# Preparing q and k of a head pair in one 128-partition cast, with both low parts on GpSimd: causal attention plus gated MLP

## The chip, the cores and the metric

One NeuronCore of a Trainium2 chip (trn2) runs the whole program. The metric is the device time of one execution in microseconds (us), here the median of three runs. TensorE is called PE, VectorE DVE, ScalarE ACT, GpSimd POOL, and SyncE, which issues all of this kernel's transfers, SP.

## The reference

Inputs are q, k, v of 8 batches x 8 heads x 576 positions x 64, a row s per head, and four MLP arrays. Cut to what matters:

```python
scores = 1/sqrt(D) * q @ k.T                        # per head, 576 x 576
cum  = np.cumsum(np.maximum(s, 0), axis=-1)
bias = -(cum[:, None] - cum[None, :])
scores = np.where(causal, -1e9, scores + np.minimum(bias, 0))
attn = softmax(scores);  x = attn @ v               # heads joined: 576 x 512 per batch
h = relu(x @ w_in);  u, g = halves(h)               # 512 -> 2 x 512
g = (g - mean(g)) / sqrt(var(g) + 1e-6)             # per position
g = w_spatial @ g + b_spatial[:, None]              # over positions, 576 x 576
out = (u * g) @ w_out
```

## The kernel before

The work is cut into 32 pairs of heads (four pairs to a batch) and eight batches of MLP. All products are done in fp16 with a value split into a high part (a cast) and a low part (value minus high part), and two or three products summed in PSUM.

**A pair's scores.** For each of the two heads PE multiplies two stacked operands of 128 rows: KA with QA, and KB with QB. Each has room for three pairs at a time (QA[i], KA[i], QB[i], KB[i], i = p % 3). Before the change QA[i] and KA[i] hold, in rows 64 to 127, the high parts of q and k, and in rows 0 to 63 the constants and three prefix rows (`cum`, split into three fp16 rows `cc`) that carry the bias; KB[i] holds the low part of k in rows 0 to 63 and the high part of k in rows 64 to 127, QB[i] the high part of q and the low part of q. The function `prepare` (L367 to L401 before the change) fills them: `load` brings k and q of a pair in one transfer (k in rows 0 to 63, q in rows 64 to 127 of `raw`, room for two); `kh` casts k on DVE (L390), `kl` subtracts on DVE (L408), `qh` casts q on ACT (L411), `ql` subtracts on POOL in four pieces (L394); `ka`, `kb` and `qb` are transfers from SBUF to SBUF that move a high part to the other half of the partitions (L404, L406, L412); `aux` puts the prefix rows in rows 61 to 63 of KA[i] with three transfers (L398). Pairs 0 to 2 are computed in fp32 from raw tiles (`native_*`) and use none of this.

**The rest of a pair** (`attend`). Scores arrive in seven PSUM banks in turn (three buffers `psS`). For each block DVE adds the mask and takes the row maximum (L462), ACT takes the exponential (L479), DVE forms the reciprocals of the row sums (L484, L485), ACT writes the high part of the scaled weights (L510), DVE the low part (L512), SP transposes the result by DMA (L519), and PE multiplies with v (L618, L625). The last 64 positions of both heads (the tail rows) share two blocks, columns 4 and 9 of the row maxima; a DVE instruction joins their two maxima (`tail_min`, L489), another their sums (`tail_sum`, L493), with reciprocals of their own.

**The MLP of a batch** (`mlp`): five gate products `vps` (L668), eight `ups` (L761), eight `sps` (L776 to L779), eight `ops` (L805), each with casts on ACT and DVE between. The inverse root of the variance is taken on POOL in two instructions (L692, L693).

**What sets the order.** Nothing is ordered by hand. Every step is added to a planner (`Plan`) with its engine, a duration, a place (a number by which ready steps of an engine are picked), what it needs, and the buffers it takes and gives. `Plan.order` plays the program through with these numbers and emits each engine's instructions in the order that comes out; each engine, SP's queue among them, then runs its list strictly in that order.

Of the kernel before, what the change touches and what calls it, by code (L numbers as in the profile page):

```python
# [27 lines left out]
class Plan:  # L28
# [17 lines left out]
    def order(self):  # L46
        import heapq
        steps, index = self.steps, self.index
        n = len(steps)
        left, users = [0] * n, [[] for _ in range(n)]  # L50
# [15 lines left out]
        dma = 0.0  # L66
# [3 lines left out]
        while len(out) < n:  # L70
            for e, heap in ready.items():
# [71 lines left out]
def attn_gated_mlp(ctx, tc, kqT, v, s, w_in, w_spT, b_sp, w_out, outT):  # L143
    nc = tc.nc
    P = 128
    NHB, D, H, S = kqT.shape
# [85 lines left out]
    def load_s():  # L232
        t = wk.tile([NH, 4 * S], F32, tag="u", bufs=1, name="cst")
        cst["raw"], cst["pos"], cst["cum"], cst["zer"] = (t[:, i * S:(i + 1) * S] for i in range(4))
        nc.sync.dma_start(out=cst["raw"], in_=s)

    add("s", SYNC, 650, -30, load_s, take=["u"], move=(0, 300))
    add("zero", DVE, 400, -29, lambda: nc.vector.memset(cst["zer"], 0.0), need=["s"])

    def prefix(k):  # L240
# [80 lines left out]
    for c in range(KC):  # L321
        for hf, at, at2 in ((1, 2.2 + 1.2 * c, 6.5 + 0.5 * c), (0, 4.5 + c, 9 + 0.5 * c)):
# [4 lines left out]
        convert(("out", c), w_out[c * P:c * P + P], wo1[:, c], wo2[:, c], "wst", "ob", 10.6 + 1.1 * c, 10.6 + 1.1 * c)  # L327

    def spatial(c):
# [11 lines left out]
        at = 11 + 0.4 * c if c < NFULL else 13  # L341
# [7 lines left out]
    def bias_rows(k):  # L349
        if k == 0:  # L350
            hold["bf"] = wk.tile([1, S], F32, tag="ob", bufs=room["ob"], name="bf")
            hold["bp"] = wk.tile([1, 3, S], F16, tag="wst", bufs=1, name="bp")
            nc.sync.dma_start(out=hold["bf"], in_=b_sp)
            return
        bf, bp = hold["bf"], hold["bp"]
        if k == 1:
            nc.vector.tensor_scalar(bf, bf, SWSP * SVN / 2048.0, None, op0=ALU.mult)
            for i in range(3):
                nc.vector.tensor_copy(bp[:, i], bf)
                if i < 2:  # L360
                    nc.vector.tensor_tensor(out=bf, in0=bf, in1=bp[:, i], op=ALU.subtract)
        else:
            for i in range(3):
                nc.sync.dma_start(out=wx2[TAIL + i:TAIL + i + 1], in_=bp[:, i])

    add("bf", SYNC, 650, 13.1, lambda: bias_rows(0), take=["ob", "wst"], move=(0, 100))
    add("bp", DVE, 2800, 13.2, lambda: bias_rows(1), need=["bf"], give=["ob"])  # L367
    add("bx", SYNC, 1950, 13.3, lambda: bias_rows(2), need=["bp", ("sl", NFULL)], move=(1300, 100), give=["wst"])

# [7 lines left out]

    def prepare(p):
        i = p % 3
        lo, hi = slice(0, 64), slice(64, 128)  # L380
        set_free = [("static", i)] + ([last(p - 3)] if p - 3 >= NNAT else [])

        def load():
            raws[p] = wk.tile([P, 2, S], F32, tag="raw", bufs=2, name=f"raw{p}")
# [504 lines left out]
```

## Time and profile before

| what | value |
|---|---|
| three runs | 726.39, 728.44, 728.59 us (median 728.44) |
| the profiled execution | 728.78 us, of which the span of its instructions is 727.0 us |
| mean granted PE clock | 0.931 of full speed |
| busy share of the span | PE 83%, DVE 88%, ACT 71%, POOL 23% |
| DMA | 72.0% of 16 engines' time, 114.81 MB |

The busy share is an average over the span, which has three stretches: up to about 200 us, in which weights are converted and PE often waits; a steady stretch, in which a batch repeats every 78.6 us; and the end, in which only the MLP is left. How the profile is read: busy time of PE is modelled from when matmuls issue; DVE and ACT are busy or idle as recorded.

### The profile page before, as it was taken

Reading aid. Unit: us, or ns where it says so; the run is one execution under the profiler, and the core shown is the slowest. Engines: PE = TensorE matmul, PEld = TensorE weight load, DVE = VectorE, ACT = ScalarE, POOL = GpSimd, SP = SyncE. Lnnn points to the kernel's source line nnn. Section 1 sums busy time; section 2 is a strip of 40 time slices with the busy share of each in tenths; the row PEclk is TensorE's granted clock in tenths of the full one; section 3 lists DMA queues with packets and bytes.
Section 4 is the critical chain, followed back from the end, with each engine's and each line's share of the span. In section 5 each row is a group of like instructions: output and inputs, shape, how many; then the busy total and the mean of one; then the engine's idle time right before and its main releaser. Section 6 shows DMA issues by size and latency. Waiting matters only on the chain.

```text
span 727.0 us, 15919 instructions
## 1 busy us (share of the span) xinstructions
PE 606.4 (83%) x5696; PEld 417.0 (57%) x5696; DVE 636.6 (88%) x1669; ACT 518.5 (71%) x1319; POOL 165.8 (23%) x217
## 2 busy tenths in 40 slices
PE   1654469647889989989889988999889988999998
PEld 0232335425656766567546765667647754777676
DVE  7999999999999998899889999999899989884531
ACT  3867777775686887787776879787777779765322
POOL 8120222202224210521124221422223122200200
PEclk9966669957999999999989999999999999999999
DMA  8896967489596789859785779968895866445001
GB/s 222 240 252 126 200 117 193 111 202 200 139 191 161 145 173 189 209 124 192 173 194 119 139 189 199 191 132 183 174 225 128 193 120 150 92 94 135 22 13 65
DMA packets 243037, 114.81 MB, mean 158 GB/s; under 512 B 213471, under 2 KB 226957, under 8 KB 242958
## 3 DMA queue, kind: packets, MB, share of 16 engines
q1 hardware_dynamic: 242958, 113.80, 72.0%
q8 instruction: 44, 0.72, 0.4%
q14 instruction: 35, 0.29, 0.1%
HBM read 37.28 MB, written 9.44 MB: 64 GB/s over the span
## 4 chain that ended last, share of the span: by engine, by line
PE 28%; DVE 25%; ACT 3%; issue 3%; POOL 1%; DMA 0%; DVEq 0%; ACTq 0%; POOLq 0%
PE ops L805 7%; PE ups L761 6%; DVE pb L512 6%; PE vps L668 5%; DVE psS L462 5%; PE sps L776 3%; PE psS L456 3%; DVE KB L408 2%; PE av L618 1%; DVE V L585 1%; DVE g L796 1%; DVE g L784 1%; ACT p L479 1%; DVE sm L484 1%; DVE mx L462 1%
## 5 line engine op out<-in xcount | busy, mean ns | idle before, releaser
L394 POOL TENSOR_TENSOR QB<-raw,QA 64x288 f16<-64x288 f32 x116 | 111.8, 993 | 327.0 <-ACT QA L411 280.6
L479 ACT ACTIVATE p<-psS,mx 128x128 f32<-128x128 f32 (+3 forms) x256 | 132.9, 524 | 57.4 <-DVE mx L462 55.0
L462 DVE CUSTOM_DVE_ANT_0 psS<-psS,mb 128x128 f32<-128x128 f32 (+1 forms) x320 | 154.9, 500 | 15.4 <-PE psS L456 10.4
L510 ACT ACTIVATE pb<-p,sm 128x384 f16<-128x384 f32 (+3 forms) x256 | 123.1, 554 | 21.1 <-issue 9.9
L456 PE MATMUL psS<-KA,QA 128*128 128x128 f16 (+1 forms) x348 | 83.6, 315 | 63.0 <-ACT p L479 62.7
L512 DVE SCALAR_TENSOR_TENSOR pb<-p,sm,pb 128x384 f16<-128x384 f32 (+3 forms) x256 | 129.8, 558 | 5.1 <-ACT pb L510 4.9
L805 PE MATMUL ops<-g,wo 128*128 128x288 f16 x768 | 106.8, 296 | 3.5 <-ACT ob L812 2.4
L668 PE MATMUL vps<-win,xt 128*128 128x512 f16 (+1 forms) x576 | 102.2, 356 | 4.8 <-ACT xt L634 3.6
L776 PE MATMUL sps<-ws,vn 128*128 128x288 f16 x768 | 104.6, 286 | 0.0
L761 PE MATMUL ups<-xt,win 128*128 128x288 f16 x768 | 102.1, 286 | 2.5 <-ACT u L766 2.4
L805 PEld LDWEIGHTS <-wo 128*128 128x128 f16 x768 | 77.2, 101 | 30.8 <-issue 5.5
L456 PE MATMUL psS<-KB,QB 128*128 128x128 f16 (+1 forms) x348 | 90.0, 313 | 2.8 <-DMA KB<-kh 2.8
L761 PEld LDWEIGHTS <-win 128*128 128x128 f16 x768 | 73.8, 98 | 27.9 <-issue 6.4
L776 PEld LDWEIGHTS <-vn 128*128 128x128 f16 x768 | 74.1, 98 | 23.3 <-issue 2.1
L668 PEld LDWEIGHTS <-xt 128*128 128x128 f16 (+1 forms) x576 | 48.4, 104 | 57.1 <-issue 10.9
L618 PE MATMUL av<-pT,V 128*64 128x128 f16 (+2 forms) x960 | 68.2, 297 | 14.4 <-DMA pT<-pb 14.4
L618 PEld LDWEIGHTS <-V 128*64 128x64 f16 x960 | 53.9, 120 | 33.5 <-issue 20.8
L456 PEld LDWEIGHTS <-QB 128*128 128x128 f16 x348 | 30.1, 104 | 61.2 <-issue 55.8
L692 POOL TENSOR_SCALAR rs<-mv 128x1 f32<-128x1 f32 x40 | 15.7, 393 | 195.3 <-DVE mv L688 194.8
L479 ACT ACTIVATION_READ_ACCUMULATOR p<-psS,mx 128x1 f32 x256 | 51.0, 199 | 0.0
L456 PEld LDWEIGHTS <-QA 128*128 128x128 f16 x348 | 29.8, 104 | 34.1 <-issue 27.0
L462 DVE DVE_READ_ACCUMULATOR2_ANT mx<- 128x1 f32 x320 | 45.0, 141 | 0.0
(82 smaller groups left out, 857.6 us busy)
## 6 DMA issues: line engine op xcount, KB each, us to landing
raw<-in_kqT_dram SPq DMA_DIRECT2D x29, 576.0 KB
out_dram<-ob SPq DMA_DIRECT2D x32, 288.0 KB
vraw<-in_v_dram SPq DMA_DIRECT2D x16, 512.0 KB
QB<-QA SPq DMA_DIRECT2D x29, 144.0 KB
KA<-kh SPq DMA_DIRECT2D x29, 144.0 KB
KB<-kh SPq DMA_DIRECT2D x29, 144.0 KB
wst<-in_w_in_dram SPq DMA_DIRECT2D x8, 512.0 KB
vraw<-in_v_dram SPq DMA_DIRECT2D x16, 128.0 KB
```

What stands on the lines that cost most here:

```text
L394: nc.gpsimd.tensor_tensor(out=QB[i][hi, j, cs], in0=raws[p][hi, j, cs], in1=QA[i][hi, j, cs], op=ALU.subtract)
L456: nc.tensor.matmul(ps[m, c0:c0 + w], U[i][:, g, q0:q0 + n], T[i][:, g, k0:k0 + w], start=st, stop=not st)
L462: nc.vector.tensor_tensor_reduce(out=ps[:, c0:c0 + w], in0=ps[:, c0:c0 + w], in1=mask, op0=ALU.add, op1=ALU.min, scale=-0.125, scalar=3.0e ...
L479: nc.scalar.activation(dst, ps[:, c0:c0 + w], AF.Exp, bias=mx[:, mcol:mcol + 1], scale=-1.0, accum_out=sm[:, col:col + 1])
L510: nc.scalar.activation(dst[:, off:off + w], src, AF.Copy, bias=0.0, scale=sc)
L512: nc.vector.scalar_tensor_tensor(out=dst[:, n + off:n + off + w], in0=src, scalar=sc, in1=dst[:, off:off + w], op0=ALU.mult, op1=ALU.subtract)
L618: nc.tensor.matmul(dst, V[i][:, jc, h + j], rhs, start=jc == n == 0 and q0 > 0, stop=jc == 3 and n == 2)
L668: nc.tensor.matmul(ps[m, 0:w], xx[:, c, t * P:t * P + (m.stop - m.start)], ww[:, c, NF + g * w:NF + g * w + w], start=c == n == 0, stop=c ...
L692: nc.gpsimd.tensor_scalar(rs, cell["mv", t][:, 1:2], 1.0e-6, 1.0 / (SVN * SVN), op0=ALU.add, op1=ALU.mult)
L761: nc.tensor.matmul(ps[:, 0:TH], ww[:, c, fs], xx[:, c, ts], start=n == 0, stop=n == 3 * KC - 1)
L776: nc.tensor.matmul(ps[:, 0:TH], vv[:, c, fs], ww[:, c, ts], start=n == 0, stop=False)
L805: nc.tensor.matmul(ps[:, 0:TH], ww[:, f, ms], gg[:, f, ts], start=n == 0, stop=n == 3 * FC - 1)
```

## The change

q and k of a pair change places in `raw` (q in rows 0 to 63 now). One ACT instruction `h` (L413) casts all 128 rows into KA[i], which puts the high part of k into rows 64 to 127 where it belongs and leaves the high part of q in rows 0 to 63. Four POOL instructions `l` (L406) form both low parts, 128 rows wide, into QB[i]. Four transfers (L409) then spread them: `qa` and `kb` copy the two high parts to QA[i] and KB[i], `kl` copies the low part of k from QB[i] to KB[i], and `qb` writes the high part of q over the place which `kl` has read. Only then does `aux` (L419) bring the three prefix rows in one transfer, from a copy `ccd` in DRAM, over rows 61 to 63 of KA[i]. DVE has no part in `prepare` any more.

```diff
-        def kh():
-            live["kh", p] = wk.tile([64, 2, S], F16, tag="kh", bufs=1, name=f"kh{p}")
-            nc.vector.tensor_copy(live["kh", p], raws[p][lo])
-        def qlo(j, c):
+        def low(j, c):
             cs = slice(c * TH, c * TH + TH)
-            nc.gpsimd.tensor_tensor(out=QB[i][hi, j, cs], in0=raws[p][hi, j, cs], in1=QA[i][hi, j, cs], op=ALU.subtract)
+            nc.gpsimd.tensor_tensor(out=QB[i][:, j, cs], in0=raws[p][:, j, cs], in1=KA[i][:, j, cs], op=ALU.subtract)
...
-        add(("ka", p), SYNC, 650, a1 + .02, lambda: nc.sync.dma_start(out=KA[i][hi], in_=live["kh", p]),
...
-        add(("kl", p), DVE, 1270, a1 + .04, lambda: nc.vector.tensor_tensor(
-            out=KB[i][lo], in0=raws[p][lo], in1=live["kh", p], op=ALU.subtract), need=[("kh", p)] + set_free)
...
-        add(("qh", p), ACT, 1150, a1 + .06, lambda: nc.scalar.copy(QA[i][hi], raws[p][hi]), need=[("load", p)] + set_free)
+        add(("h", p), ACT, 1060, a1, lambda: nc.scalar.copy(KA[i], raws[p]), need=[("load", p)] + set_free)
         for k in range(4):
-            add(("ql", p, k), POOL, 930, a1 + .08 + .01 * k, lambda k=k: qlo(k // 2, k % 2), need=[("qh", p)])
+            add(("l", p, k), POOL, 690, a1 + .01 * k, lambda k=k: low(k // 2, k % 2), need=[("h", p)],
+                give=["raw"] if k == 3 else ())
+        move("qa", a1 + .01, QA[i][bot], KA[i][top], [("h", p)])
+        move("kb", a1 + .02, KB[i][top], KA[i][bot], [("h", p)])
+        add(("aux", p), SYNC, 500, a1 + .03, lambda: nc.sync.dma_start(
+            out=KA[i][61:64], in_=ccd[2 * p:2 * p + 2].rearrange("h r s -> r h s")), need=["ccd", ("qb", p), ("qa", p)], move=(0, 30))
+        move("kl", a1 + .04, KB[i][bot], QB[i][bot], lows)
+        move("qb", a1 + .05, QB[i][bot], KA[i][top], [("kl", p)])
```

The tail rows are chained. The second tail block's row maximum starts from the first one's instead of a constant, so `tail_min` is gone; the tail's exponentials wait for that block. The tail's sums are joined first, and the reciprocals of the second head and of the tail are taken together over five columns, so the high parts of the second head wait for the tail's exponentials:

```diff
-                                               op0=ALU.add, op1=ALU.min, scale=-0.125, scalar=3.0e38,
+                                               op0=ALU.add, op1=ALU.min, scale=-0.125,
+                                               scalar=mx[:, 4:5] if col == 9 else 3.0e38,
...
-            add(("sum", p, j), DVE, 170, at + .01, lambda j=j: over_sums(5 * j, 5 * j + 4),
-                need=[("exp", p, j, ic) for ic in range(4)])
+            add(("sum", p, j), DVE, 300, at + X["sum"], lambda j=j: over_sums(4 * j, 4 + 5 * j),
+                need=[("exp", p, j, ic) for ic in range(4)] + ([("tsum", p)] if j else []))
...
-            over_sums(4, 5)
```

Small work at the start changes engines: the split of the prefix rows (`cc`, L246 to L249) and of the bias row (`bp`, L357 to L361) and one memset go from DVE to POOL. The first of the two instructions of the inverse root goes from POOL to DVE. And the planner is given other numbers: a table X of places for nearly every kind of step, some other durations, and a rule by which a DVE and a POOL step, but for kinds that it names, are not played at the same time:

```diff
+    APART = {"red", "xl", "gm", "bn", "mv", "mb", "mb4", "static", "zero"}
...
-                    if all(room[t] > 0 and lines[t][-1] == i for t in steps[i][6]):
+                    if all(room[t] > 0 and lines[t][-1] == i for t in steps[i][6]) and (port <= now or not shared[i]):
...
+X = {"load": -5.2, "prep": -2.2, "vf": -0.5, "vc": 1.5, "red": 0.0, "exp": 0.092, "sum": -0.172, "hi": -0.219, ...}
```

What this does to the lists is shown at two places. The first is DVE at the start of the program, up to the instruction that releases the first matmul (`qraw<-sel`, the selector rows of pair 0). Before:

```order
L243 TENSOR_SCALAR cst<-cst 64x576
L244 SCALAR_TENSOR_TENSOR cst<-cst 64x576
L270 COPY kraw_116<-cst 64x576 x2
L270 COPY kraw_118<-cst 64x576 x2
L246 CAST cc<-cst 64x576
L247 TENSOR_TENSOR cst<-cst,cc 64x576
L248 CAST cc<-cst 64x576
L249 TENSOR_TENSOR cc<-cst,cc 64x576
L390 CAST kh_170<-raw_130 64x1152
L408 TENSOR_TENSOR KB_85<-raw_130,kh_170 64x1152
L266 COPY qraw_140<-sel 64x1152
```

Now:

```order
L254 TENSOR_SCALAR cst<-cst 64x576
L255 SCALAR_TENSOR_TENSOR cst<-cst 64x576
L308 COPY kraw_119<-cst 64x576 x2
L308 COPY kraw_121<-cst 64x576 x2
L304 COPY qraw_146<-sel 64x1152
```

The split of the prefix rows and the work on pair 3 no longer stand ahead of the selector rows.

The second place is SP's list for one pair in the steady stretch (76, 85, 82, 73 and 77, 86, 83, 74 are the numbers of the KA, KB, QB, QA tiles of one i). Before:

```order
L519 DMA_TRANSPOSE pT_0_4344<-pb_4287 128x20x128
L398 DMA KA_76<-cc 1x2x576 x3
L404 DMA KA_76<-kh_4454 64x1152
L406 DMA KB_85<-kh_4454 64x1152
L412 DMA QB_82<-QA_73 64x1152
L386 DMA raw_4520<-in_kqT_dram 128x1152
L519 DMA_TRANSPOSE pT_1_4525<-pb_4472 128x20x128
L519 DMA_TRANSPOSE pT_None<-pb_15_4499 128x10x128
```

Now:

```order
L409 DMA QA_74<-KA_77 64x1152
L409 DMA KB_86<-KA_77 64x1152
L409 DMA KB_86<-QB_83 64x1152
L402 DMA raw_2898<-in_qkT_dram 128x1152
L522 DMA_TRANSPOSE pT_1_2906<-pb_2815 128x20x128
L522 DMA_TRANSPOSE pT_None<-pb_10_2887 128x10x128
L409 DMA QB_83<-KA_77 64x1152
L578 DMA vraw_2978<-in_v_dram 128x4x256
L579 DMA vraw_2978<-in_v_dram 128x256
L522 DMA_TRANSPOSE pT_0_3042<-pb_3005 128x20x128
L419 DMA KA_77<-ccd 3x2x576
```

The third transfer (`kl`) now waits for POOL with the transposes of the pair behind it; between it and `qb`, and between `qb` and `aux`, stand one or two transposes.

## Rows read from the trace of the kernel before

**Rows 1.** The page, part 1: busy time, share of the span and instructions of each engine over the whole span.
```profile
PE 606.4 (83%) x5696; PEld 417.0 (57%) x5696; DVE 636.6 (88%) x1669; ACT 518.5 (71%) x1319; POOL 165.8 (23%) x217
```
**Rows 2.** Busy time of each engine in five stretches: the head, the steady stretch, the two halves of one batch (gate and up products, then mixing and down products), and the end. Columns: stretch and its length, busy us and count of PE, of PE's weight loads, of DVE, ACT and POOL, granted PE clock, DMA share, GB/s.
```profile
0.00:200.00 200.00, 118.61 (x971) 76.23 (x972) 189.95 (x463) 137.08 (x333) 47.63 (x63) 0.81 0.80 182
200.00:609.95 409.95, 374.12 (x3684) 258.85 (x3683) 382.25 (x1029) 321.64 (x835) 108.38 (x134) 0.97 0.80 170
374.06:405.05 30.99, 30.99 (x256) 19.27 (x256) 26.95 (x68) 21.67 (x57) 9.72 (x14) 0.94 0.65 147
405.05:451.95 46.90, 41.58 (x460) 30.52 (x456) 45.05 (x128) 39.19 (x105) 11.25 (x12) 1.00 0.87 171
660.34:727.00 66.66, 63.27 (x532) 46.54 (x530) 21.72 (x46) 21.96 (x50) 4.73 (x10) 0.99 0.19 54
```
**Rows 3.** The chain of work that ended last, in order of time (start us, length us, what): a transfer in it, the first gate products of two batches three apart, the products of the last batch, and one pair's weights times v.
```profile
366.12 2.40 DMA KB<-kh
374.06 13.86 PE vps L668 x72
389.93 1.76 PE av L618 x30
391.69 0.47 PE avt L625 x30
...
609.95 11.90 PE vps L668 x72
...
686.23 11.87 PE ups L761 x96
698.09 1.47 PE sps L776 x12
...
711.85 11.78 PE ops L805 x96
```
**Rows 4.** PE in order of time: the last four score matmuls of a pair, 512 columns each, two for either half of the output partitions, and what follows them.
```profile
404.86 0.38 PE L456 MATMUL psS<-KA,QA 128*64 128x512 f16 x2
405.08 0.38 PE L456 MATMUL psS<-KB,QB 128*64 128x512 f16 x2
405.29 1.80 PE L618 MATMUL av<-pT,V 128*64 128x384 f16 x30
```
**Rows 5.** DVE instructions by line and shape from 374.06 to 609.95 us, three batches: count, busy us and mean ns of one, then idle time before them.
```profile
L408 DVE TENSOR_TENSOR KB<-raw,kh 64x1152 f16<-64x1152 f32 x12 | 17.6, 1464 | 0.0
L390 DVE CAST kh<-raw 64x1152 f16<-64x1152 f32 x12 | 8.8, 735 | 0.0
L489 DVE TENSOR_TENSOR mx<-mx 128x1 f32<-128x1 f32 x12 | 3.4, 286 | 0.3
L485 DVE RECIPROCAL sm<-sm 128x1 f32<-128x1 f32 x12 | 2.0, 164 | 0.4
L484 DVE TENSOR_SCALAR sm<-sm 128x1 f32<-128x1 f32 x12 | 1.8, 154 | 0.4
```
**Rows 6.** The same for the head, 0 to 200 us.
```profile
L408 DVE TENSOR_TENSOR KB<-raw,kh 64x1152 f16<-64x1152 f32 x8 | 11.1, 1390 | 0.1
L390 DVE CAST kh<-raw 64x1152 f16<-64x1152 f32 x8 | 6.5, 812 | 0.0
L359 DVE CAST bp<-bf 1x576 f16<-1x576 f32 x3 | 2.2, 730 | 0.1
L361 DVE TENSOR_TENSOR bf<-bf,bp 1x576 f32<-1x576 f32 x2 | 1.9, 958 | 0.1
L249 DVE TENSOR_TENSOR cc<-cst,cc 64x576 f16<-64x576 f32 x1 | 1.2, 1173 | 0.0
L246 DVE CAST cc<-cst 64x576 f16<-64x576 f32 x1 | 0.9, 901 | 0.0
```
**Rows 7.** Durations on POOL and DVE over the whole span: first two rows with least/median/largest ns, then two memsets of different widths by line and shape (busy us, mean ns).
```profile
L394 POOL TENSOR_TENSOR QB<-raw,QA x116: 727/736/3915, 10.6 to 603.4; 64x288 f16<-64x288 f32 x116
L408 DVE TENSOR_TENSOR KB<-raw,kh x29: 1318/1343/1828, 13.2 to 600.8; 64x1152 f16<-64x1152 f32 x29
...
L222 POOL MEMSET QA<- 64x576 f32 x3 | 1.9, 647 | 0.1
L206 POOL MEMSET mb<- 128x640 bf16 x1 | 0.6, 626 | 0.0
```
**Rows 8.** The start in order of time: SP's issue of the q transfer of pair 0, DVE's selector rows, the first matmul with what it waited for.
```profile
4.28 0.47 SPq L263 DMA_DIRECT2D qraw<-in_kqT_dram  x1
...
14.88 0.74 DVE L266 COPY qraw<-sel 64x1152 f32<-64x1152 f32 x1
...
15.68 9.66 PE L453 MATMUL psS<-kraw,qraw 128*128 128x128 f32 x30 [15.68 <-DVE qraw L266]
```
**Rows 9.** What SP spends on issuing one transfer, least/median/largest ns: the two sizes of transpose, the prefix rows, a move of one half.
```profile
L519 SPq DMA_TRANSPOSE pT<-pb x64: 2986/3251/5782, 31.4 to 662.7; - x64
L519 SPq DMA_TRANSPOSE pT_None<-pb x32: 1271/1356/1541, 40.2 to 665.8; - x32
L398 SPq DMA_DIRECT2D KA<-cc x87: 558/589/1603, 14.7 to 602.9; - x87
L404 SPq DMA_DIRECT2D KA<-kh x29: 466/533/649, 20.0 to 603.5; - x29
```
**Rows 10.** What PE waited for from 200 to 610 us: total us, times, longest us; the longest of the list.
```profile
PE psS L456 <- ACT p L479: 29.7, 19, 3.4
```

More of the change, by code (lines that the diff above doesn't have):

```diff
@@ L49, in order @@
         n = len(steps)
+        shared = [x[1] in (DVE, POOL) and (x[0] if isinstance(x[0], str) else x[0][0]) not in self.APART for x in steps]
         left, users = [0] * n, [[] for _ in range(n)]
@@ L65, in order @@
         free = dict.fromkeys(ready, 0.0)
-        dma = 0.0
+        dma = port = 0.0
         events, now, out = [], 0.0, []
@@ L230, in attn_gated_mlp, with open_s @@
     cst = {}
[L232 to L238, printed above, removed]
+    def open_s():
+        t = wk.tile([P, 4 * S], F32, tag="u", bufs=1, name="cst")
+        cst["raw"], cst["pos"], cst["cum"], cst["zer"] = (t[0:NH, i * S:(i + 1) * S] for i in range(4))
+        cst["b"] = t[64:65, 0:S]
+        cst["bp"] = t[64:65, S:4 * S].bitcast(F16)[:, 0:3 * S].rearrange("p (i s) -> p i s", s=S)
+    add("s0", SYNC, 0, -31, open_s, take=["u"])
+    add("s", SYNC, 650, -30, lambda: nc.sync.dma_start(out=cst["raw"], in_=s), need=["s0"], move=(0, 300))
+    add("zero", POOL, 600, -29, lambda: nc.gpsimd.memset(cst["zer"], 0.0), need=["s0"])
     def prefix(k):
@@ L347, in attn_gated_mlp @@
         spatial(c)
[L349 to L368, printed above, removed]
     BLK = (2, 0, 3, 6)
@@ L400, in prepare @@
-        a0, a1 = (2 * p - 5.2, 2 * p - 1.2) if p > 3 else (0.5, 2.1)
-        add(("load", p), SYNC, 500, a0, load, take=["raw"], move=(0, 2130))
-        add(("aux", p), SYNC, 1950, a1, aux, need=["cc"] + set_free, move=(1300, 30))
-        add(("kh", p), DVE, 670, a1 + .01, kh, need=[("load", p)], take=["kh"])
-        add(("ka", p), SYNC, 650, a1 + .02, lambda: nc.sync.dma_start(out=KA[i][hi], in_=live["kh", p]),
-            need=[("kh", p)] + set_free, move=(0, 540))
-        add(("kb", p), SYNC, 650, a1 + .03, lambda: nc.sync.dma_start(out=KB[i][hi], in_=live["kh", p]),
-            need=[("kh", p)] + set_free, move=(0, 540))
@@ L422, in attend @@
         ready = [("nsel", p), ("ncum", p, 0), ("ncum", p, 1)] if p < NNAT else \
-            [("aux", p), ("ka", p), ("kb", p), ("kl", p), ("qb", p)] + [("ql", p, k) for k in range(4)]
+            [("aux", p), ("qa", p), ("kb", p), ("kl", p), ("qb", p)]
         def jobs(b):
@@ L537, in attend @@
                 tk = ["p32"] if k == 0 and b in (0, 3) else ["q32"] if ic == 4 else []
[L538 to L539 removed]
+                add(("exp", p, j, ic), ACT, 50 + act(w), at + X["exp"] + .001 * k, lambda b=b, k=k: weights(b, k),
+                    need=[("red", p, 6 if ic == 4 else b)] + first, take=tk,
                     give=[bank] if k == len(ics) - 1 else ())
[L541 removed]
@@ L560, in attend @@
+        add(("tlo", p), DVE, dve(640), t5 + X["tlo"], lambda: split(None, 0, True), need=[("thi", p)], give=["q32"])
+        add(("tturn", p), SYNC, 1600, t5 + X["tturn"], lambda: turn(None), need=[("tlo", p)], take=["pT4"], give=["pb4", "mx"],
             move=(625, 1850))
@@ L654, in mlp @@
         cell = {}
-        place = [8 * b + 10.3 + 8 / NU * k for k in range(NU)]
+        place = [8 * b + X["m0"] + (X["mb0"], X["mb1"], 0, 0, 0, 0, 0, 0)[b] + X["span"] / NU * k for k in range(NU)]
         xs = [("xl", 4 * b + k, 0) for k in range(4)] + [("xl", 4 * b + 3, 1)]
@@ L737, in mlp @@
             need = [("bn", b, t)]
             if tail:
-                add(("swap", b), SYNC, 1300, at + .015, swap, need=need, move=(650, 50))
+                add(("swap", b), SYNC, 1300, at + X["bn"] + .005, swap, need=need, move=(650, 50))
                 need = [("swap", b)]
-            add(("mv", b, t), DVE, 80, at + .02, lambda t=t: spread(t), need=need)
-            add(("rs", b, t), POOL, 900, at - 3, lambda t=t: root(t), need=[("mv", b, t), "mb4"])
-            add(("nm", b, t), DVE, 460 if not tail else 323, at + .03, lambda t=t: normalise(t), need=[("rs", b, t)], give=["st"])
@@ L744, in mlp @@
-            add(("vh", b, t, 0), ACT, act(w) - 90, at + .04, lambda t=t: vhigh(t),
+            add(("mv", b, t), DVE, 270, at + X["bn"] + .01, lambda t=t: spread(t), need=need)
+            add(("rs", b, t), POOL, 640, at - 3, lambda t=t: root(t), need=[("mv", b, t), "mb4"])
+            add(("nm", b, t), DVE, 460 if not tail else 323, at + X["nm"], lambda t=t: normalise(t), need=[("rs", b, t)], give=["st"])
+            add(("vh", b, t, 0), ACT, act(w) - 90, at + X["vh"], lambda t=t: vhigh(t),
```

154 lines of the change are left out of this document (86 added, 68 removed).

## The prediction

> **What bounds the kernel now.** I read the page first: DVE is the busiest engine, 88% of the span against 83% of PE [rows 1]. An average over unlike stretches decides nothing, so the table by stretches comes next [rows 2]. In the head DVE works 189.95 of 200 us while PE runs at a mean granted clock of 0.81: the head is DVE's. At the end (from 660 us) DVE works 21.72 of 66.66 us and PE 63.27: the end is PE's, and DVE time taken out there is worth nothing. Between them a batch repeats: its gate products start at 374.06 and, three batches on, at 609.95 [rows 3], so 78.6 us a batch. That stretch has to be read by halves. In the first (gate and up products) PE is busy without a gap, 30.99 of 30.99 us; in the second (mixing and down products) DVE is busy 45.05 of 46.90 us, 96%, and PE 41.58 [rows 2]. So DVE time is worth its full length in the head and in the second half of each batch, until PE takes over.
>
> **Where PE takes over.** The last batch runs with little else beside it and gives PE's prices: `vps` 11.90, `ups` 11.87, `sps` from 698.09 to 711.85, that is 13.76, `ops` 11.78, together 49.3 us [rows 3]. A column of `ups` costs 11.87/(96 x 288) = 0.43 ns. A pair's scores move 2 x 2 x 1280 columns for the heads, and the tail as if it were 1280 more: its two halves run side by side, as four matmuls of 512 columns take 405.29 - 404.86 = 0.43 us [rows 4], what two would. 6400 x 0.43 ns = 2.75 us. Weights times v take 1.76 + 0.47 = 2.23 us [rows 3]. A batch: 49.3 + 4 x 4.98 = 69.2 us of PE. The second half holds 69.2 - 31.0 = 38.2 us of it and now takes 46.9.
>
> **The change part by part.**
>
> DVE, each pair: `kl` 1.464, `kh` 0.735, `tail_min` 0.286, the tail's own two reciprocal steps 0.164 + 0.154, together 2.80 us [rows 5]. A batch loses 11.2 us and gains the first root instruction five times; the trace has it only on POOL, so I price it as the 128x1 TENSOR_SCALAR of DVE, 0.154 us [rows 5], 0.8 in all. The second tail block's maximum now starts from a number that the instruction before it has just written; no row shows such a read, its ends are 0 and the 0.286 of the instruction that it replaces, and I take 0. Net 10.4 us of the 26.95 + 45.05 = 72.0 us of that batch [rows 2].
>
> Steady stretch: the first half stays, because PE has no gap there. The second half holds 46.9/77.9 of the batch's time; by that share it loses 6.3 us, so DVE needs 45.05 - 6.3 = 38.8 us, PE 38.2. Two engines with equal loads that feed each other in fixed order do not both run without gaps. The nearest row for what the leading engine manages is this same half, 45.05/46.90 = 0.96: 38.8/0.96 = 40.4 us, a gain of 6.5 us a batch. From 200 to 609.95 us there are 5.2 batches: **34 us**. Ends of this term: 46.9 - 38.8 = 8.1 us a batch (42 us) if nothing gaps, and 2 us a batch (10 us) for the case that latency rules, below.
>
> Head: DVE loses `kl` 11.1, `kh` 6.5, `bp` 2.2 + 1.9, `cc` at least 1.2 + 0.9 [rows 6], and for eight pairs the tail's three at 0.60 us [rows 5], 4.8; it gains five root instructions, 0.8. Net 27.8 us. Of this 1.2 + 0.9 and one `kh` and `kl` (together some 4.3 us by their means) stand ahead of the selector rows, which release the first matmul at 15.68 [rows 8]. What DVE no longer does there it may spend waiting for the q of pair 0, whose transfer is issued at 4.28; when that lands no row shows. The gain there lies between 0 and 4.3; I take 0.5, as the transfers ahead of it are nearly the same. Head: **24 us**, ends 23 and 28.
>
> POOL: `l` replaces `ql` one for one, 116 instructions, twice as many partitions and as many elements in each. No row shows this subtraction 128 wide. Its ends are the present 0.736 us and twice that. I take the lower: the memsets of 64 x 576 and 128 x 640 cost 0.647 and 0.626 us [rows 7], so the width does not show there. `cc` and `bp` come to POOL near the start, where it has time; pair 3, which needs `cc`, has three native pairs ahead of it.
>
> What the pieces wait for: a quiet `ql` takes 0.736 us, the longest 3.915; `kl` of DVE 1.318 to 1.828 [rows 7]. So instructions of these two engines do hold each other up. The Trainium skill (SBUF — State Buffer, section Who interferes with whom) says why: a DVE instruction with two SBUF inputs and a GpSimd instruction that reads SBUF exclude each other for a whole instruction. The longest times above agree with that. If `l` keeps the length of `ql`, the change takes 58 DVE instructions out of this contest and adds none in the steady stretch, so I add nothing for it; the other case is a rival.
>
> ACT: `h` for `qh`, the same 1152 elements a partition: nothing. SP, each pair: two prefix transfers fewer (2 x 0.589), one move more (0.533): 0.6 us less [rows 9]. A batch of 78.6 us holds 8 x 3.25 + 4 x 1.36 + 12 x 0.589 + 12 x 0.533 = 44.9 us of these, after the change 42.3; other transfers are the same. The moved bytes grow by 144 KB a pair; at 170 GB/s for a share of 0.80 [rows 2], that is some 0.7 us of full DMA time a pair, and a batch goes from 0.80 x 78.6 = 63 to 66 of 72 us: 0.91, below full, so nothing, but little is left.
>
> The chain from `load` to the scores grows: `h`, four `l` (2.9 us), then `kl`, `qb`, `aux`, one after the other landing, at about 2.4 us each [rows 3], some 11 us; for `aux`, which now comes from DRAM, no row shows the landing, and I take the same. Its cover is that QA to KB hold three pairs: two pair periods of 19.6 us. The chained tail makes the second head's high parts wait for two more exponentials; its cover is the three steps to the product with v, which PE does not wait for in the steady stretch: its one long list entry is the score banks waiting for ACT [rows 10].
>
> **Sum.** 727.0 - 24 - 34 = 669 us of span; the profiled execution took 728.78, 1.8 more than its span, and lies 0.3 above the median of the runs: 671 us.
>
> **The rivals.**
>
> *PE without gaps*: the new order closes the second half to 38.8 us and the start gains too. 42 + 28: 727 - 70 + 1.8 = 659; if DVE's work moves into the first half and PE's 38.2 holds in the second, 8.7 x 5.2 + 28 = 73, so 656. For it: PE has no gap in the first half even now. Against: equal loads. Chance 0.17.
>
> *Latency, not DVE's load, sets the second half*: PE's waits there are score banks that ACT has not emptied, 29.7 us from 200 to 610 [rows 10], a turn of maximum, exponential and next scores through three banks. If that turn stays as long, a batch gains 2 us: 727 - 24 - 10 + 1.8 = 695. Against: DVE idles only 4% of that half, so the turn is long because DVE is late. Chance 0.15.
>
> *The wide subtraction takes twice as long*: 16 x 0.736 = 11.8 us more of POOL a batch, in which DVE's two-input instructions wait. If half of it reaches DVE, its batch falls by 4.5 instead of 10.4 us, 2.7 in the second half: 5.2 x 2.8 = 15 us, and the head gains about 12: 702. The Trainium skill (GPSIMD Engine Reference, section Elementwise — side-by-side cycle accounting) speaks against the move of `kl`: GpSimd needs about twice DVE's time for a two-input elementwise operation. The rows agree for equal shapes: 4 x 0.736 = 2.94 us on POOL against 1.34 on DVE [rows 7]. It costs here only if the rows of k do not ride along. Chance 0.06.
>
> *Slower: SP's queue becomes the bound.* `kl` waits for POOL in the middle of SP's list, with transposes behind it, and `qb` and `aux` for landings. With none of it covered, a pair adds 2.94 + 2 x 2.4 = 7.7 us of waiting, a batch 31 us. Priced transfers are 42.3 us a batch; the other 20 (loads, outputs, the MLP's tail), at a move's 0.533, are 11. 53 + 31 = 84 us, over 78.6: 5.2 x 5.4 = 28 us lost against 24 won, 733. It decides once the uncovered wait passes 78.6 + 4.6 - 53 = 30 us a batch (4.6: what the head's 24 us pay for). Against: in SP's list the landings are covered by transposes of 3.25 and 1.36 us, so only `kl`'s wait is bare, 2.94 less two moves, 1.9 us a pair, 7.5 us a batch. Chance 0.04.
>
> That the change does not do what it says can be excluded for DVE: its list is 126 instructions shorter and holds no `kh` or `kl`.
>
> **How the numbers follow.** Forecast 0.56, the four rivals 0.17, 0.15, 0.06, 0.04, and 0.02 for an even result from a mixture. A measurement of this kernel tells 0.3% (2.2 us) from no change. The range runs from 654 (PE without gaps, less the 2.2 us by which the runs differ) to 702 (both middle rivals); outside lie the slower case, the even one, and the far edges. Faster 0.94, same 0.02, slower 0.04.
>
> **What would show it.** In the profile after: DVE near 550 us busy; a batch near 72 us, its first half still 31 us; the second near 40 us with PE and DVE both above 93%; the POOL subtraction near 0.74 us when quiet; the first 200 us of work done by about 176. A POOL median near 1.5 us, a batch above 76 us, or SP idle ahead of `kl` with PE waiting for transposes would make me wrong. PE above 97% in the second half would make the gain larger.

## The result and the profile after

The changed kernel takes 675.78 us (median of four runs, 675.35 to 676.87), the kernel before 728.52 (four runs, 726.39 to 728.72): a ratio of 0.9285, 95% interval 0.9264 to 0.9305. Forecast were 671 us and a range of 654 to 702. The profiled execution has a span of 674.0 us against 727.0.

The page after, part 1 (answers to [rows 1]) and the transfers' queue of part 3:
```profile
PE 593.3 (88%) x5696; PEld 408.7 (61%) x5696; DVE 570.7 (85%) x1544; ACT 508.8 (75%) x1319; POOL 137.0 (20%) x188
...
q1 hardware_dynamic: 245271, 118.30, 81.2%
```
DVE lost 65.9 us and POOL 28.8; PE is now the busiest engine. The clock's mean rose from 0.931 to 0.959.

The span is compared by landmarks, the starts of the batches' first gate products. Busy time after by stretches, columns as in [rows 2]: up to the second batch's gate products, five batches from there, one of these in two halves, cut at the end of its last up product, the seventh batch and the last:
```profile
0.00:186.28 186.28, 123.36 (x1081) 77.58 (x1081) 171.49 (x430) 140.57 (x349) 54.81 (x73) 0.85 0.94 209
186.28:553.49 367.21, 354.37 (x3563) 248.13 (x3561) 329.21 (x925) 303.81 (x806) 75.59 (x105) 1.00 0.90 191
406.26:438.97 32.71, 30.49 (x262) 19.26 (x259) 30.35 (x83) 26.28 (x69) 6.38 (x9) 1.00 0.82 187
438.97:479.60 40.63, 40.29 (x455) 30.35 (x454) 35.47 (x103) 34.52 (x94) 8.70 (x12) 1.00 0.96 205
553.49:620.78 67.29, 66.27 (x683) 47.53 (x681) 52.50 (x151) 48.56 (x132) 2.95 (x5) 1.00 0.63 124
620.78:674.00 53.22, 49.33 (x378) 35.48 (x375) 17.47 (x41) 15.87 (x35) 3.68 (x5) 1.00 0.09 32
```
The same five batches of the kernel before, the batch of [rows 2] in two halves with the same cut (0.5 us earlier than there), and the seventh batch:
```profile
211.89:609.88 397.99, 365.02 (x3570) 252.19 (x3568) 371.48 (x1004) 311.82 (x810) 103.88 (x130) 0.97 0.80 169
374.06:404.58 30.52, 30.52 (x250) 19.01 (x248) 26.75 (x67) 21.43 (x56) 9.72 (x14) 0.94 0.66 150
404.58:451.95 47.37, 42.05 (x466) 30.77 (x464) 45.25 (x130) 39.42 (x105) 11.25 (x12) 1.00 0.86 170
609.88:674.27 64.39, 64.39 (x672) 46.53 (x669) 47.86 (x143) 43.91 (x118) 5.01 (x10) 1.00 0.52 108
```
The 53.0 us come from three places. The stretch up to the second batch is 25.6 us shorter (211.89 to 186.28), five batches 30.8 (397.99 to 367.21, or 79.6 to 73.4 a batch), and the end is 3.4 longer: the seventh batch takes 553.49 to 620.78, 67.3 us instead of 64.4, the last 53.2 instead of 52.7. In the second half PE is now busy 40.29 of 40.63 us, 99%; the first is 2.2 us longer than in that batch of before, with as much idle time on PE.

What PE waited for in those five batches (us in total, times, longest), where [rows 10] had the score banks with 29.7 us (26.9 of it in the same five batches):
```profile
PE ups L764 <- ACT u L769: 7.2, 5, 1.4
```
and the place of that wait in one batch, PE in order of time, the idle time and its releaser in brackets:
```profile
433.45 1.63 PE L764 MATMUL ups<-xt,win 128*128 128x288 f16 x12 [1.43 <-ACT u L769]
435.44 0.38 PE L463 MATMUL psS<-KA,QA 128*128 128x512 f16 x1 [0.36 <-ACT p L487]
```
The score banks' wait has all but gone (4.9 us); once a batch an up product waits for ACT's u.

The start (answers to [rows 8]), the selector rows on DVE and the first matmul:
```profile
9.36 1.15 DVE L304 COPY qraw<-sel 64x1152 f32<-64x1152 f32 x1
...
11.83 4.49 PE L460 MATMUL psS<-kraw,qraw 128*128 128x128 f32 x8 [11.83 <-DMA qraw<-in_qkT_dram]
```
PE starts 3.9 us sooner, now released by the transfer of q.

The new subtraction on POOL, least/median/largest ns (answers to [rows 7]):
```profile
L406 POOL TENSOR_TENSOR QB<-raw,KA x116: 722/732/1252, 24.6 to 550.1; 128x288 f16<-128x288 f32 x116
```
Twice the partitions take the same time, 732 ns against 736.

### The profile page after: what moved, and what is told of

It is laid out like the page before. It is cut to its first block, busy times and chain, and to the rows that moved or that the text cites. A ratio compares the mean times of both kernels' runs of the same rounds, so it can differ in the third digit from the quotient of the medians.

```text
span 674.0 us, 15717 instructions
## 1 busy us (share of the span) xinstructions
PE 593.3 (88%) x5696; PEld 408.7 (61%) x5696; DVE 570.7 (85%) x1544; ACT 508.8 (75%) x1319; POOL 137.0 (20%) x188
## 5 line engine op out<-in xcount | busy, mean ns | idle before, releaser
L406 POOL TENSOR_TENSOR QB<-raw,KA 128x288 f16<-128x288 f32 x116 | 89.6, 802 | 299.8 <-ACT KA L413 299.7
L469 DVE CUSTOM_DVE_ANT_0 psS<-psS,mb 128x128 f32<-128x128 f32 (+3 forms) x288 | 134.5, 475 | 8.2 <-PE psS L463 2.8
L808 PE MATMUL ops<-g,wo 128*128 128x288 f16 x768 | 101.5, 286 | 0.7 <-ACT ob L815 0.7
L670 PE MATMUL vps<-win,xt 128*128 128x512 f16 (+1 forms) x576 | 99.0, 348 | 0.1
L764 PEld LDWEIGHTS <-win 128*128 128x128 f16 x768 | 73.9, 98 | 33.0 <-issue 11.2
L808 PEld LDWEIGHTS <-wo 128*128 128x128 f16 x768 | 74.5, 98 | 25.0 <-issue 2.7
L779 PEld LDWEIGHTS <-vn 128*128 128x128 f16 x768 | 74.3, 98 | 24.2 <-issue 2.1
L620 PE MATMUL av<-pT,V 128*64 128x128 f16 (+2 forms) x960 | 63.1, 285 | 8.0 <-DMA pT<-pb 5.5
L696 POOL TENSOR_TENSOR rs<-rs,mhalf 128x1 f32<-128x1 f32 x40 | 24.8, 619 | 199.4 <-DVE rs L692 175.0
L620 PEld LDWEIGHTS <-V 128*64 128x64 f16 x960 | 49.2, 115 | 26.4 <-issue 14.7
L463 PEld LDWEIGHTS <-QA 128*128 128x128 f16 x348 | 30.2, 102 | 37.2 <-issue 29.9
L460 PE MATMUL psS<-kraw,qraw 128*128 128x128 f32 (+5 forms) x72 | 23.5, 553 | 27.4 <-ACT p L487 14.0
```

The costliest lines, as they stand in the source:

```text
L406: nc.gpsimd.tensor_tensor(out=QB[i][:, j, cs], in0=raws[p][:, j, cs], in1=KA[i][:, j, cs], op=ALU.subtract)
L463: nc.tensor.matmul(ps[m, c0:c0 + w], U[i][:, g, q0:q0 + n], T[i][:, g, k0:k0 + w], start=st, stop=not st)
L469: nc.vector.tensor_tensor_reduce(out=ps[:, c0:c0 + w], in0=ps[:, c0:c0 + w], in1=mask, op0=ALU.add, op1=ALU.min, scale=-0.125, scalar=mx[: ...
L620: nc.tensor.matmul(dst, V[i][:, jc, h + j], rhs, start=jc == n == 0 and q0 > 0, stop=jc == 3 and n == 2)
L670: nc.tensor.matmul(ps[m, 0:w], xx[:, c, t * P:t * P + (m.stop - m.start)], ww[:, c, NF + g * w:NF + g * w + w], start=c == n == 0, stop=c ...
L696: nc.gpsimd.tensor_tensor(out=rs, in0=rs, in1=mhalf, op=ALU.pow)
```

## The experiments

Ratios are to the kernel before, run on the same chip; its median there lay between 726.33 and 729.19 us, so small differences are read from the ratios. "A batch" is the mean of the five between the second and the seventh gate products, with the DVE and PE busy time of one.

| kernel | us | ratio, 95% interval | a batch | DVE | PE |
|---|---|---|---|---|---|
| before | 728.52 | 1 | 79.6 | 74.3 | 73.0 |
| changed | 675.78 | 0.9285 (0.9264 to 0.9305) | 73.4 | 65.8 | 70.9 |
| 1 old places | 689.32 | 0.9475 (0.9441 to 0.9508) | 74.5 | 65.5 | 71.1 |
| 2 old prepare | 724.36 | 0.9979 (0.9950 to 1.0008) | 78.8 | 73.5 | 72.0 |
| 3 prepare alone | 697.37 | 0.9572 (0.9530 to 0.9615) | 75.3 | 65.6 | 71.7 |
| 4 DVE time back | 724.50 | 0.9960 (0.9942 to 0.9978) | 80.2 | 73.3 | 72.5 |
| 5 less DVE, other order | 690.72 | 0.9477 (0.9440 to 0.9515) | 76.5 | 64.1 | 72.4 |
| 6 less PE | 671.95 | 0.9217 (0.9187 to 0.9247) | 72.8 | 65.3 | 67.1 |
| 7 POOL twice | 711.50 | 0.9761 (0.9728 to 0.9795) | 77.5 | 69.3 | 71.6 |
| 8 old tail | 687.33 | 0.9430 (0.9377 to 0.9483) | 74.3 | 66.1 | 71.0 |
| 9 less DVE, same order | 673.91 | 0.9278 (0.9257 to 0.9299) | 73.1 | 63.5 | 70.8 |
| 10 less DVE and PE | 666.77 | 0.9176 (0.9146 to 0.9207) | 72.0 | 63.0 | 67.2 |
| 11 no loads of v | 676.51 | 0.9316 (0.9301 to 0.9332) | 73.5 | 65.9 | 70.9 |
| 12 half of POOL | 672.48 | 0.9257 (0.9237 to 0.9277) | 72.7 | 63.3 | 70.7 |

The theory was the prediction's: DVE time is the price, in the head and in each batch, until PE takes over. The rivals: the gain is the planner's new places; it is the tail's new chain; the batch is now held by transfers, by POOL or by no single engine.

### Which part carries the gain (runs 1, 2, 3)

Run 1 is the changed kernel with the numbers of the old program in the table of places (and in `attend`'s place of the products with v):
```diff
-X = {"load": -5.2, "prep": -2.2, ... "exp": 0.092, "sum": -0.172, "hi": -0.219, "lo": -0.36, ...
+X = {'load': -5.2, 'prep': -1.2, ... 'exp': 0.0, 'sum': 0.01, 'hi': 0.02, 'lo': 0.02, ...
```


> The changed kernel with the places that the kernel before had (its planner rule and everything else as changed). DVE theory (DVE's time taken out of the head and of the second half of each batch is the gain, until PE is the bound): the relief stays, 676 to 692 us, a batch under 75.5. Placement theory (the new table of places made most of the gain): 705 us or more, a batch of 77 or more.

Run 2 is the changed kernel with `prepare` as it was:
```diff
-        add(("h", p), ACT, 1060, a1, lambda: nc.scalar.copy(KA[i], raws[p]), ...
+        add(("kh", p), DVE, 670, a1 + .01, kh, need=[("load", p)], take=["kh"])
+        add(("kl", p), DVE, 1270, a1 + .04, ...
+        add(("qh", p), ACT, 1150, a1 + .06, lambda: nc.scalar.copy(QA[i][hi], raws[p][hi]), ...
...
```


> The changed kernel with the preparation of before (k cast and subtracted on DVE, q on ACT and POOL, prefix rows in three transfers), places and all else as changed. DVE theory: 29 x 2.2 us of DVE come back, 715 to 728 us, the second half of a batch near 46 us again. Placement theory: 680 to 695 us.

Run 3 is the kernel before with the new `prepare` alone, the same edit the other way round.

> The kernel before with the new preparation alone (one cast, low parts on POOL, four moves, prefix rows from DRAM). DVE theory: 17.6 of the head's 27.8 us and 8.0 of a batch's 10.4 us are kh and kl, so 683 to 698 us. Placement theory: 712 us or more. SP theory (its list with the new wait becomes the bound without new places): above 728.

All three came out as the theory of DVE's time expects. With the old `prepare` nothing of the gain is left that can be told: places, tail and the small work at the start are worth nothing without the new one. The new `prepare` alone brings 4.3% of the 7.2, and the batch follows DVE down from 74.3 to 65.6 us busy. On top of it all the rest brings 2.9%; of that the places are 1.9% (run 1 against the changed kernel, 13.5 us). So the parts do not add up: what is worth nothing by itself is worth 2.9% once DVE is relieved. Run 3 has nearly the changed kernel's DVE time a batch, 65.6 us, and needs 1.9 us more for it: that is what the rest (places, planner's rule, tail) is worth in a batch.

### Is it DVE's time? (run 4)

The two operations that left DVE come back, with nobody reading them, everything else as changed:
```diff
+        def dk():
+            nc.vector.tensor_copy(spare[bot], raws[p][bot])
+        def dl():
+            nc.vector.tensor_tensor(out=spare[bot], in0=raws[p][bot], in1=spare[bot], op=ALU.subtract)
...
+        add(("dk", p), DVE, 670, a1 + .01, dk, need=[("load", p)])
+        add(("dl", p), DVE, 1270, a1 + .04, dl, need=[("dk", p)])
```


> The changed kernel with two DVE instructions a pair added that nobody reads, of the kind and size of those taken out (a cast and a subtraction, 64 x 1152), planned like the others. DVE theory: DVE goes from 90 to about 98% in the steady stretch and bounds it again, 705 to 728 us. If the path through DVE mattered and not its time: 676 to 685 us.

The two in run 4, busy us and mean ns, by line and shape:
```profile
L413 DVE TENSOR_TENSOR spare<-raw,spare 64x1152 f16<-64x1152 f32 x29 | 41.9, 1447 | 0.9
L410 DVE CAST spare<-raw 64x1152 f16<-64x1152 f32 x29 | 25.3, 873 | 0.9
```
These 67.2 us (56.5 of busy time, for a reason given below) cost 48.7 us, though no instruction reads their results: SP's moves, the one prefix transfer and the wide cast are all still there. A batch goes from 73.4 to 80.2 us for 7.5 more of DVE, 0.9 us per us. That lies within the first theory's 705 to 728 us: most of the gain is DVE's time. The price itself is not clean: `raw` is held until the two are done, and the order is planned anew, and runs 5 and 9 below lie 0.020 (14.5 us) apart by the order alone. Run 7, with the order kept, points the same way: its batches have 3.4 us more of DVE and are 4.0 us longer, though there the low parts also come later.

### Where does it stop? (runs 5, 6, 9, 10)

Runs 5 and 9 leave out the low part of v from the third half batch on; the products read an old one. Run 5 takes the step out of the plan, run 9 only the instruction, so that each engine's order stays that of the changed kernel:
```diff
+            if hb < 2:
                 nc.vector.scalar_tensor_tensor(
                     out=V2[i], in0=vraws[hb], scalar=SV, in1=V1[i], op0=ALU.mult, op1=ALU.subtract)
```
Run 6 leaves out one of the three mixing products, with the order kept; run 10 does both:
```diff
-                for vv, ww in ((vn1, ws1), (vn1, ws2), (vn2, ws1)):
+                for vv, ww in ((vn1, ws1), (vn2, ws1)):
```


> The changed kernel without the DVE instruction that forms the low part of v for 14 of the 16 half batches (stale low parts are used; 1.5 us each, 3 us a batch). If PE now bounds the steady stretch: 667 to 676 us, a batch no shorter than 72.5. If DVE still does: a batch falls by up to 3 us, 655 to 662 us.

> The changed kernel without one of the three products of the mixing step (32 matmuls of 288 columns a batch, 3.9 us; that product is left out of the result), same order. If PE bounds: 3.4 to 3.9 us a batch in six batches and the end, 643 to 655 us. If DVE or the transfers bound the second half: 668 us or more, but for the 3.9 us of the last batch.

> The changed kernel without the low part of v (the V2 = SV*vraw - V1 pass on VectorE) from the third half batch on; the mixing products read the old low part, so nothing leaves PE, and each engine's order is otherwise that of the changed kernel. About 1.5 us x 2 of VectorE a batch is left out, 14 passes in all, some 21 us. If VectorE's chain bounds the 73.3-us batch: a batch of 70.3 to 71.5 us and 656 to 666 us. If transfers, SyncE's list or PE bound it: a batch of 72.8 to 73.4 us and 671 to 677 us.

> The changed kernel without the low part of v from the third half batch on (as in the run before) and without one of the three mixing products (32 matmuls, 3.9 us of PE a batch), the order otherwise that of the changed kernel. If PE and VectorE bound a batch together, each as soon as the other is relieved: a gain larger than the sum of the two single ones, 640 to 658 us. If VectorE alone bounds it: the sum of the singles, 652 to 663 us. If neither (transfers): 668 to 675 us.

Run 5 missed by 15 us upwards and decides nothing: the planner, with a step less, emitted another order (batches of 73.7 to 78.1 us). Hence run 9. Five batches of runs 6, 9 and 10, a fence each, columns as above:
```profile
189.17:553.19 364.02, 335.65 (x3403) 232.42 (x3401) 326.47 (x920) 300.78 (x803) 75.63 (x105) 1.00 0.89 192
621.40:670.70 49.30, 45.39 (x346) 32.32 (x343) 16.83 (x41) 15.75 (x35) 3.68 (x5) 0.99 0.10 35
```
```profile
187.40:553.02 365.62, 353.86 (x3562) 246.82 (x3560) 317.41 (x915) 304.34 (x807) 75.62 (x105) 1.00 0.89 192
```
```profile
184.55:544.60 360.05, 336.03 (x3402) 232.45 (x3400) 315.16 (x913) 302.46 (x806) 75.73 (x105) 1.00 0.90 195
```
PE 18.7 us shorter in these batches makes them 3.2 us shorter; DVE 11.8 shorter, 1.6; both, 7.2. The last batch of run 6, where PE works alone, gives the whole 3.9 us back (53.22 to 49.30), so the product is worth its length where PE is the bound, and not in the steady batches. So runs 6 and 9 come out where neither PE nor DVE alone bounds a batch; run 9 as a whole can't be told from the changed kernel. Run 10 falls between its cases. Its gain on the changed kernel, 0.0109 of the ratio, can't be told from the 0.0075 of the two single runs with intervals of 0.002 to 0.003 to either side; the 7.2 us against 4.8 above come from one execution each, that of run 10 the fastest of its four (663.69 us). Either way it is far from what two engines that bound together would give. Where run 6's PE time went, its waits in those batches:
```profile
PE psS L463 <- ACT p L487: 18.0, 19, 1.4
PE ups L764 <- ACT u L769: 6.8, 5, 1.4
PE sps L779 <- DVE g L787: 3.6, 5, 0.7
```
The score banks' wait came back, 4.9 to 18.0 us. By these waits the turn of row maximum (DVE), exponential (ACT) and next scores (PE) stands behind PE's list, less than 1 us a batch away; no run shortened that turn, so this is a reading, not a test.

### Transfers and POOL (runs 7, 11, 12)

Run 7 makes each low part twice; run 12 leaves it out for a pair's second head from the seventh pair on; run 11 leaves out the loads of v from the third half batch on. The order stays that of the changed kernel.
```diff
+            for _ in range(2):
                 nc.gpsimd.tensor_tensor(out=QB[i][:, j, cs], in0=raws[p][:, j, cs], in1=KA[i][:, j, cs], op=ALU.subtract)
```
```diff
+            if p >= 6 and j == 1:
+                return
```
```diff
+            if hb > 1:
+                vraws[hb] = vraws[1]
+                return
```


> The changed kernel with each POOL subtraction done twice, planned as one (116 more of 0.73 us, 85 us of POOL). If POOL holds DVE up for whole instructions: DVE's two-input instructions lengthen, half of 85 us in sum or more, and with 10% of DVE idle the time is 685 to 705 us. If the two hardly meet: 675 to 680 us.

> The changed kernel without the low parts of q and k for the second head of each pair from the seventh pair on (52 GpSimd subtractions of 0.73 us, 38 us in all; the products read the old low parts). By the price of the run that doubled them (35.7 us for 85 to 104 us more of GpSimd, 0.35 to 0.42 us each): 13 to 16 us less, 659 to 663 us. If GpSimd's subtractions cost VectorE nothing unless they pile up: 673 to 677 us.

> The changed kernel without the transfers of v from the third half batch on (the tile of the second is read again, so every engine computes as before); 1.28 MB less a batch of some 14 MB, and 28 issues less on SyncE's list. If the DMA engines bound the second half of a batch (share 0.97 there): a batch 3 to 6 us shorter, 645 to 660 us. If VectorE's chain bounds it: a batch of 72.5 to 73.4 us, 670 to 677 us.

Five batches of run 11:
```profile
187.74:555.06 367.32, 354.42 (x3562) 247.69 (x3560) 329.63 (x925) 304.38 (x807) 75.59 (x105) 1.00 0.82 174
```
The DMA share falls from 0.90 to 0.82 and the five batches stay at 367 us: transfers' load does not bound the batch. (SP's list, which keeps most of its entries, is not excluded by this.)

Run 7 loses 35.7 us, somewhat more than expected. DVE instructions by shape over its whole span, and the same of the changed kernel behind it (count, busy us, mean ns):
```profile
L516 DVE SCALAR_TENSOR_TENSOR pb<-p,sm,pb 128x512 f16<-128x512 f32 x64 | 54.9, 857 | 0.3 <-ACT pb L514 0.3
L470 DVE CUSTOM_DVE_ANT_0 psS<-psS,mb 128x512 f32<-128x512 f32 x64 | 44.4, 693 | 0.8 <-PE psS L461 0.7
L494 DVE RECIPROCAL sm<-sm 128x5 f32<-128x5 f32 x32 | 6.1, 191 | 1.1
```
```profile
L515 DVE SCALAR_TENSOR_TENSOR pb<-p,sm,pb 128x512 f16<-128x512 f32 x64 | 48.8, 763 | 0.3 <-ACT pb L513 0.3
L469 DVE CUSTOM_DVE_ANT_0 psS<-psS,mb 128x512 f32<-128x512 f32 x64 | 44.4, 694 | 1.0 <-PE psS L460 0.7 <-PE psS L463 0.2
L493 DVE RECIPROCAL sm<-sm 128x5 f32<-128x5 f32 x32 | 6.1, 191 | 1.1
```
The low parts of the weights, with two operands in SBUF, become longer; the row maxima, whose scores lie in PSUM, and the reciprocals do not. So POOL holds up certain forms and not all of DVE. This agrees with the Trainium skill (SBUF — State Buffer, section Who interferes with whom), by which only certain forms of DVE instruction share a port pair with GpSimd.

Run 12 shows the other side. One form of DVE instruction in five batches of run 12, and the same of the changed kernel:
```profile
L494 DVE TENSOR_SCALAR sm<-sm 128x5 f32<-128x5 f32 x20 | 3.4, 171 | 0.7
```
```profile
L492 DVE TENSOR_SCALAR sm<-sm 128x5 f32<-128x5 f32 x20 | 8.4, 419 | 0.7
```
With half of POOL's subtractions gone it takes 171 ns. The 419 of the changed kernel are a mean of two lengths: ten of the twenty take 171 or 172 ns and ten 664 to 672, close to a subtraction's 732, with none between. In all, DVE's five batches fall from 329.21 to 316.65 us with not one of their 925 instructions removed, for 29.9 us of POOL: 0.42 us per us. Yet the five batches fall by only 3.8 us, and the whole kernel from 675.78 to 672.48 with intervals that overlap. The 13 to 16 us expected from run 7's price missed: here too DVE time below the present 65.8 us a batch is worth little (0.30 us per us).

### The tail's chain (run 8)

```diff
-                                               scalar=mx[:, 4:5] if col == 9 else 3.0e38,
+                                               scalar=3.0e38,
...
+        add(("tmin", p), DVE, 100, t5, tail_min, need=[("red", p, 5), ("red", p, 6)])
```


> The changed kernel with the tail rows unchained (joined maximum and own reciprocals again, 0.6 us of DVE a pair, 2.4 us a batch). DVE theory: little in the steady stretch, which PE bounds now, some 5 us in the head: 677 to 684 us. Latency theory (the chained tail makes the second head wait, undoing it helps): 668 to 674 us.

It is above both expectations, but its batches are uneven (73.0, 77.5, 70.4, 79.1, 71.6 us): it is planned anew with places made for the chained tail. It does not tell what the chain is worth. Its batch of 70.4 us shows no lower floor either: it stands between two of 77.5 and 79.1, and the five average 74.3.

## Why the prediction was right, and where not

**The bound.** Right where it carries the sum: DVE time sets head and batch (run 4, with its reservations). Put side by side, a batch follows DVE at 0.9 us per us from 73.3 us of DVE (run 4) to 65.8 (changed), and at 0.13 from there to 63.5 (run 9); where between 73.3 and 65.8 it bends no run shows.

**Head: 24 us, measured 25.6.** Within its ends of 23 and 28. The start gave 3.9 us, where the prediction took 0.5 from a range of 0 to 4.3: DVE's selector rows are done at 10.51 and q lands 1.3 us later. So the rest of the head gave 21.7 us where 23.5 was forecast, and that the sum is so near is in part two errors of opposite sign.

**Steady stretch: 34 us, measured 30.8 for five batches** (5 x 6.5 = 32.5 by the prediction). The size was nearly right, in part by luck. The 6.5 us were worked out on the batch of 77.9 us from 374 us on; after the change a batch takes 73.3 to 73.9, 4.0 to 4.6 less. The mean of the five comes out at 6.2 only because that of the kernel before, 79.6, holds one of 86.26 us; the other four average 77.9. The working under the 6.5 failed in three places:

- "The first half stays, because PE has no gap there." By the end of the last up product it grew from 30.52 to 32.71 us, with 2.2 us of gaps; over the five batches it had lain between 29.3 and 33.7 us and now lies at 32.7 or 32.8.
- The second half came to 40.63 us, and 40.4 was forecast, but on another road. Of DVE 38.8 us were to stay there and be 96% of it; DVE lost 9.8 us there and gained 3.6 in the first half, and its 35.47 are 87%. PE was priced at 38.2 us and is busy 40.29, 99%. The 38.2 are 69.2 less 31.0, the one taken at a granted clock of 0.99, the other at 0.94 [rows 2]; and PE needs 70.9 us a batch, not 69.2. The prediction said that PE above 97% there would make the gain larger. It is above, and the gain is not larger.
- "Until PE takes over": the page agrees, but run 6 does not. With 3.7 us of PE less a batch falls 0.6 us. Relieving PE or DVE alone gives almost nothing, both together 1.4 us a batch of the 3.7 removed from PE.

What sets 72 us in run 10, with PE busy 93% and DVE 88%, stays open. No run took work off ACT or off SP's list, and a cycle through the fixed orders of several engines fits as well.

The prediction priced no clock. For nearly the same matmuls of five batches (3570 and 3563) PE was busy 365.02 us before, at a granted clock of 0.97, and 354.37 after, at 1.00, the level of 2.4 GHz throughout. Before, PE waited for score banks just ahead of the batch from 374 us on:
```profile
370.16 0.22 PE L456 MATMUL psS<-KA,QA 128*128 128x128 f16 x1 [1.67 <-ACT p L479]
372.27 0.59 PE L456 MATMUL psS<-KA,QA 128*128 128x512 f16 x1 [1.52 <-ACT p L479]
```
That batch's gate products took 13.86 us at a clock of 0.86, those at 609.95 us 11.90 [rows 3] at 1.00. With the waits gone the clock stayed up, and PE had 10.7 us less to do in the five batches. How much of that shortened a batch no run separates; run 4's price holds some of it too (362.74 us of PE for 3563 matmuls, at 0.98).

**DVE's total: near 550, measured 570.7.** The instructions went as counted, and nearly as long as counted; the step that failed is the unit. The prediction adds up mean durations and takes the sum off busy time, but DVE's records overlap, as these two of the changed kernel do (the second starts 0.08 us before the first ends):
```profile
13.91 0.30 DVE L469 CUSTOM_DVE_ANT_0 psS<-psS,mb 128x128 f32<-128x128 f32 x1 [0.34 <-PE psS L460]
14.13 0.14 DVE L469 DVE_READ_ACCUMULATOR2_ANT mx<- 128x1 f32 x1
```
Added up one by one, the durations in five batches fell from 442.6 to 389.1 us, 10.7 a batch where 10.4 was forecast; busy time, which counts an overlap once, fell by 42.3, 8.5 a batch. Some of the rows, three of before and two of after:
```profile
L408 DVE TENSOR_TENSOR KB<-raw,kh 64x1152 f16<-64x1152 f32 x20 | 29.1, 1456 | 0.0
L390 DVE CAST kh<-raw 64x1152 f16<-64x1152 f32 x20 | 15.5, 773 | 0.0
L484 DVE TENSOR_SCALAR sm<-sm 128x4 f32<-128x4 f32 x40 | 12.6, 315 | 1.9 <-ACT p L479 1.7
L492 DVE TENSOR_SCALAR sm<-sm 128x4 f32<-128x4 f32 x20 | 3.3, 167 | 2.9 <-ACT p L487 2.9
L717 DVE TENSOR_TENSOR vn<-hv,vn 128x512 f16<-128x512 f32 x20 | 18.1, 903 | 1.7 <-ACT vn L713 1.7
```
The contest with POOL, of which the prediction said that the change "adds none in the steady stretch", has moved and not gone: the scalings of the softmax's sums together fell from 15.7 to 11.7 us, while the fp16 pieces of the MLP (`vn`) rose from 14.1 to 18.1. The root instruction took 3.8 us as priced. The maximum that starts from the one before it, taken at 0 with 0.286 as the other end, costs 0.064 (758 ns against 694), and 2.2 us of waiting in the five batches.

**POOL: the wide subtraction at 0.736 us** was right (0.732), so its rival is out. "Latency sets the batch" (695) is out as well. **SP's queue** (733) did not come: PE waited for transfers for 0.6 us in all in the five batches.

**DMA: a share of 0.91, forecast; 0.90 measured**, and run 11 confirms that it costs nothing.

**The end**: priced at no change, it is 3.4 us longer. PE is busy 49.33 of 53.22 us in the last batch, as before. The seventh grew from 64.4 to 67.3, with PE busy 66.27 instead of 64.39: 64 score matmuls start in it, 52 before, so work of the last pair has moved there. Why was not tried.

So 1.6 us more in the head, 3.2 less in the batches and 3.4 lost at the end make the 5 us between the forecast span of 669 and the 674.0 measured.

## What to carry to other kernels

Where two engines are near to equal, a price per us of busy time holds for the stretch on which it was measured: here 0.9 us per us on the way down to 65.8 us of DVE, 0.13 below. A full share of an engine in half of a batch is no proof that shortening it pays, since another turn can stand right behind it; take some of its work out in the same order and look whether the batch moves. Durations that are added up are not busy time where records overlap: 53.5 us of the one were 42.3 of the other. And an experiment that lets a planner run again compares orders, not costs: runs 5 and 9 leave out the same instructions, and their ratios lie 0.020 apart.

## What was not expected of the hardware

- A POOL subtraction of 128x288 takes 732 ns, of 64x288 736: twice the partitions did not lengthen it, and the work of `kl` added nothing to POOL's instructions.
- Doubling POOL's subtractions lengthens some DVE instructions and not others: 763 to 857 ns for two operands in SBUF at 128x512, 694 to 693 with the scores in PSUM. A scaling of 128x5 with one operand takes 171 ns with half of the subtractions left out and 419 with all, while a reciprocal of that size stays at 191 when they are doubled.
